# A decode step with two branches on one core: another cut of w_out, another way of turning the attention's output, another store

## The chip, the cores and the metric

The kernel runs on one core of a Trainium2 chip. The metric is the device time of one execution in microseconds (us); the figure for a kernel is the median of its runs. One further execution is recorded by the hardware profiler, and all durations below come from that one.

## The reference

One token (x, 1 x 576) goes through a layer norm and then through two branches in parallel; their results are added to x.

```python
xn = layernorm(x)
# branch A: cached attention, 32 query heads, 16 key/value heads of 128, the last W = 4096 positions
q = xn @ wq                                   # 576 x 4096
p = softmax(q k^T * 128**-0.5); o = p v       # two query heads share one k and v
A = o.reshape(4096) @ wo                      # 4096 x 576
# branch B: gated MLP
z = gelu(xn @ w_in)                           # 576 x 4608
g = w_sp * layernorm(z[2304:]) + b_sp         # one token: w_sp and b_sp are one number each
B = (z[:2304] * g) @ w_out                    # 2304 x 576
out = x + A + B
```

All inputs and the output are bfloat16. Some 51 MB are read from memory, most of it k and v.

## The kernel before, in words

Everything is loaded once, by SP, in the order of the list `order` (L105): w_q, the k and v of pairs of heads ("k0" to "k7", "v0" to "v7", 2 MB each), w_in in three pieces, and between and behind them w_o in four pieces ("wo0" to "wo3") and w_out. Eight buffers (`units`) are shared by all these loads, so a load waits for the release of an old buffer, and the issue lies well ahead of the landing. The schedule is written by hand: each engine runs its instructions in the order of the program text.

The list ends with "v6", "v7", "wout1", "wo3", "wout2". `wout_parts` (L104) cuts w_out, whose 2304 rows are held as 18 rows per partition: "wout1" is rows 0 to 7, "wout2" three pieces with rows 8 to 13, 14 to 16 and 17.

Heads are worked on in four groups (j = 0 to 3) of two pairs. `T` transposes k on PE (TensorE), `S` forms scores, `sm_max`, `sm_tr`, `sm_exp` and `sm_rec` the softmax, `PV` the products with v into `o_ps` (128 x 512, four blocks of 128 columns; a row has its own values in one of the four blocks). The loop over j and t (L468) puts the steps of three groups into each other, then `parts` places `turn`, `O_perm` and `WO` of earlier groups between the steps of the softmax.

`turn(j)` (L305) brings `o_ps` into the layout in which heads are columns: DVE copies it to `ov`, four fp32 products with columns of the 0/1 matrix `grp` pick the right rows of each block and add them up in `ot`, and DVE multiplies by the softmax's reciprocal sums into `oTn`. `O_perm(j)` (L316) spreads this over the partitions as w_o's rows lie (eight products, a masked product and a reduction on DVE), giving `oP`. `WO(j)` (L332) multiplies by one piece of w_o: 24 products with one column each, through `out_mm` (L327). `out_mm` adds into `out_ps`, whose three rows, on partitions 0, 32 and 64, hold 192 of the 576 outputs each.

`z_all`, `gelu`, `z_gate` and `z_rows` compute branch B up to `hv`, the vector that w_out multiplies; `hv` is there long before the end.

The end of the program (L509 to L523): the last eight steps of `PV`, rows 0 to 3 of w_out, `turn(3)`, rows 4 to 7, `O_perm(3)`, `WO(3)`, rows 8 to 17; then DVE copies the 65 partitions 0 to 64 of `out_ps` to `res`, and SP stores partitions 0, 32 and 64 of it, 384 bytes each.

Of the kernel before, what the change touches and what calls it, by code (L numbers as in the profile page):

```python
# [8 lines left out]
FP32 = mybir.dt.float32  # L9
BF16 = mybir.dt.bfloat16  # L10
ALU = mybir.AluOpType
# [3 lines left out]
P = 128  # L15
D = 576
HQ = 32
HKV = 16
DH = 128
# [10 lines left out]
NCG = 3  # L30
OW = D // NCG
PW = 28
NWO = 4
FR = FH // P
# [6 lines left out]
def kernel(  # L41
# [14 lines left out]
    nc = tc.nc  # L56
    ctx.enter_context(tc.manual_schedule())

    const = ctx.enter_context(tc.tile_pool(name="const", bufs=1))
    work = ctx.enter_context(tc.tile_pool(name="work", bufs=2))  # L60
# [14 lines left out]
    kn, vn, wq_t, win_t, wo_t, wout_t = {}, {}, {}, {}, {}, {}  # L75
# [25 lines left out]
        wo_t[j] = t  # L101

    win_parts = {1: (0, 3), 2: (3, 6), 3: (6, 9)}
    wout_parts = {1: (0, 8), 2: (8, 14, 17, 18)}  # L104
    order = ["wq1", "k0", "k1", "wq2", "k2", "k3", "v0", "v1", "win1", "win2", "win3", "k4", "k5", "v2", "v3", "wo0",  # L105
             "k6", "k7", "v4", "v5", "wo1", "wo2", "v6", "v7", "wout1", "wo3", "wout2"]
    for what in order:
        name, n = what.rstrip("0123456789"), what[-1]
# [45 lines left out]
    out_ps = ps_c.tile([P, OW], FP32, name="out_ps")  # L154
# [8 lines left out]
    for j in range(NS):  # L163
# [11 lines left out]
                                   op0=ALU.mult, op1=ALU.add, accum_out=stat[:, 1:2])  # L175
# [49 lines left out]
    o_ps = ps_o.tile([P, 4 * DH], FP32, name="o_ps")  # L225
# [67 lines left out]
    def PV(m):  # L293
        b, k = divmod(m, NCH // 2)
        j, i = divmod(b, 2)
        for g in range(4):
            w = 8 * g + 4 * i + k
            t = 4 * (4 * k + g)
            nc.tensor.matmul(o_ps[32 * g:32 * g + 32, :], lhsT=pz[j % 2][:, w, 16 - 16 * i:48 - 16 * i],  # L299
                             rhs=vn[b][:, t:t + 4, :].rearrange("p t d -> p (t d)"), start=i == 0 and k == 0,  # L300
                             stop=i == 1 and k == 3, skip_group_check=True, tile_position=(0, 32 * g))
# [1 line left out]


    def turn(j):  # L305
        ov = work.tile([P, 4 * DH], FP32, name=f"ov{j}", tag="ov")
        nc.vector.tensor_copy(ov[:], o_ps[:])  # L307
        ot = ps_m.tile([P, 8], FP32, name=f"ot{j}", tag="m")
        for t in range(4):
            nc.tensor.matmul(ot[:].rearrange("p (i c) -> p i c", i=2), lhsT=ov[:, DH * t:DH * (t + 1)],  # L310
                             rhs=grp[:].rearrange("p (i t c) -> p t i c", i=2, t=4)[:, t], start=t == 0, stop=t == 3)
        with nc.allow_low_precision(reason="the attention's output is bfloat16 in the reference"):
            nc.vector.tensor_tensor(out=oTn[:, 8 * j:8 * j + 8], in0=ot[:], in1=sm[j]["rm"][:], op=ALU.mult)  # L313

    def O_perm(j, n=1):
        op = ps_m.tile([P, 8, 8 * n], FP32, name=f"op{j}", tag="m")  # L316
        for r in range(8):
            nc.tensor.matmul(op[:, r, :], lhsT=selr[:, r, :, :].rearrange("p n q -> p (n q)"),
                             rhs=oTn[:, 8 * j:8 * j + 8 * n], start=True, stop=True)
        for k in range(n):  # L320
            tmp = work.tile([P, 8, 8], FP32, name=f"om{j + k}", tag="om")
            nc.vector.tensor_tensor(out=tmp[:], in0=op[:, :, 8 * k:8 * k + 8], in1=hm[:].unsqueeze(1).to_broadcast([P, 8, 8]), op=ALU.mult)
            with nc.allow_low_precision(reason="one of the eight is not zero, and it is a bfloat16 value"):
                nc.vector.tensor_reduce(out=oP[:, j + k, :], in_=tmp[:], axis=AXX, op=ALU.add)  # L324

    def out_mm(lhsT, rhs, start=False, last=False):
        for g in range(NCG):  # L327
            nc.tensor.matmul(out_ps[32 * g:32 * g + 1, :], lhsT=lhsT, rhs=rhs[:, OW * g:OW * (g + 1)],  # L328
                             start=start, stop=last, tile_position=(0, 32 * g))

    def WO(j):
        for r in range(8):  # L332
            out_mm(oP[:, j, r:r + 1], wo_t[j][:, D * r:D * (r + 1)])


    hv = const.tile([P, FR], BF16, name="hv")
# [74 lines left out]
    for n in range(NCH):  # L411
# [4 lines left out]
    grp = const.tile([P, 32], FP32, name="grp")  # L416
    nc.vector.tensor_reduce(out=grp[:], in_=ident_f[:].rearrange("p (g x) -> p x g", g=4), axis=AXX, op=ALU.add)
    sel = const.tile([P, 8], FP32, name="sel")
    nc.vector.tensor_reduce(out=sel[:].rearrange("p (i c) -> p i c", i=2),
                            in_=grp[:].rearrange("p (i t c) -> p i c t", i=2, t=4), axis=AXX, op=ALU.add)  # L420
    sel_neg = const.tile([P, 8], FP32, name="sel_neg")
    nc.vector.tensor_scalar(out=sel_neg[:], in0=sel[:], scalar1=1.0, scalar2=-NEG, op0=ALU.subtract, op1=ALU.mult)
    sel_t = const.tile([8, P], FP32, name="sel_t")
# [29 lines left out]
    for g in range(NCG):  # L453
        nc.tensor.matmul(out_ps[32 * g:32 * g + 1, :], lhsT=one_bf[:, 0:1], rhs=x_row[:, OW * g:OW * (g + 1)],
                         start=True, stop=False, tile_position=(0, 32 * g))
# [12 lines left out]
    for j in range(1, NB // 2):  # L468
# [23 lines left out]
        for k, what in enumerate(parts[j - 1]):  # L492
            if what == "z":
                z_all()
            elif what == "perm0":
                O_perm(0, 2)
            elif what == "perm2":
                O_perm(2)
            elif what[:4] == "turn":
                turn(int(what[4]))  # L500
            else:
                WO(int(what[2]))
            if k == 0:
                sm_exp(j)
            elif k == 1:
                sm_rec(j)
            if what == "z":
                G, sz = gelu()
    for m in range(NCH * 3, NCH * 4):  # L509
        PV(m)  # L510
    for r in range(4):
        out_mm(hv[:, r:r + 1], wout_t[r])
    turn(3)
    for r in range(4, 8):
        out_mm(hv[:, r:r + 1], wout_t[r])
    O_perm(3)
    WO(3)
    for r in range(8, FR):
        out_mm(hv[:, r:r + 1], wout_t[r], last=r == FR - 1)

    res = const.tile([P, OW], BF16, name="res")
    nc.vector.tensor_copy(res[0:32 * NCG - 31, :], out_ps[0:32 * NCG - 31, :])
    nc.sync.dma_start(out.flatten_outer_dims().rearrange("o (g c) -> (o g) c", g=NCG), res[0:32 * NCG - 31:32, :])  # L523


# [28 lines left out]
```

## Time and profile before

| what | value |
|---|---|
| median of 3 runs | 129.73 us (129.59 to 129.79) |
| the profiled execution | 129.77 us, its span 128.02 us |
| busy: PE, PE's weight loads, DVE, ACT | 68%, 48%, 47%, 23% |
| loads | 51 MB, mean 399 GB/s over the span |
| mean granted clock of TensorE | 0.85 |
| store: issue to the end of the span | 125.14 to 128.02 us |

The span is the time from the first to the last instruction in the trace; the execution's own time is 1.75 us longer. PE is TensorE, DVE is VectorE, ACT is ScalarE, SP is the engine that issues the loads and the store. In a timeline line the columns are start, length, engine, line, operation, result and sources, count; the bracket gives the idle time of the engine before it and what ended it.

### The profile page before, as it was taken

What the parts mean: (1) busy time and instruction counts of PE and PEld (TensorE: products, weight loads), DVE (VectorE), ACT (ScalarE), POOL (GpSimd) and SP (SyncE); (2) the same over time, 40 slices, a digit from 0 to 9 for tenths busy, and PEclk for the clock granted to TensorE, in tenths of its full rate; (3) what the DMA queues carried; (4) which work ended last, traced back from release to release, by engine and by line L of the source; (5) the groups of instructions that cost most, each with busy time, mean ns of one, the idle gap of its engine ahead of it and who ended that gap; (6) DMA issues with size and microseconds to landing.
All of it is one profiled execution on the core that took longest, in us unless ns stands there. A gap on an engine that the chain in (4) does not pass through costs nothing.

```text
span 128.0 us, 2605 instructions
## 1 busy us (share of the span) xinstructions
PE 86.7 (68%) x1141; PEld 61.3 (48%) x1141; DVE 60.2 (47%) x157; ACT 29.7 (23%) x39; POOL 10.2 (8%) x12
## 2 busy tenths in 40 slices
PE   2110996678895973247519969965999994697870
PEld 2110596634773621112319947624795643652640
DVE  6867157853679651002363675553365543402100
ACT  4000057320553410001200373512055432000000
POOL 7994000000000000000000000000000000000000
PEclk9999999999999999655555699999599999757755
DMA  4999999999999999999999999999999999999930
GB/s 123 430 394 445 430 451 388 436 420 450 430 415 412 433 410 436 445 405 430 461 420 410 415 427 427 435 440 415 420 425 415 423 437 425 425 414 420 400 133 0
DMA packets 4486, 51.11 MB, mean 399 GB/s; under 512 B 507, under 2 KB 636, under 8 KB 1020
## 3 DMA queue, kind: packets, MB, share of 16 engines
q1 hardware_dynamic: 4470, 50.96, 94.6%
q8 instruction: 9, 0.15, 0.5%
q10 hardware_dynamic: 6, 0.00, 0.0%
q14 instruction: 1, 0.01, 0.0%
HBM read 50.96 MB, written 0.00 MB: 398 GB/s over the span
## 4 chain that ended last, share of the span: by engine, by line
DMA 40%; PE 34%; DVE 15%; ACT 6%; issue 2%; POOL 0%; POOLq 0%; SPq 0%
DMA win<-in_B_w_in_dram 22%; PE tp L233 16%; DMA wout<-in_B_w_out_dram 15%; ACT kT L235 4%; DMA ws<-in_B_w_sp_dram 4%; PE s L250 3%; PE out_ps L328 3%; PE ot L310 2%; PE o_ps L299 2%; DVE ident_f L132 2%; DVE kT L237 2%; PE q_ps L343 1%; DVE twice L159 1%; PE za L343 1%; ACT p L275 1%
## 5 line engine op out<-in xcount | busy, mean ns | idle before, releaser
L233 PE MATMUL tp<-ident,k 128*128 128x128 bf16 x512 | 36.8, 233 | 3.6 <-ACT kT L235 1.9
L233 PEld LDWEIGHTS <-k 128*128 128x128 bf16 x512 | 33.0, 105 | 9.7 <-issue 9.6
L237 DVE COPY kT<-tp 128x1024 bf16<-128x1024 bf16 x40 | 27.0, 688 | 18.0 <-PE tp L233 17.7
L235 ACT COPY kT<-tp 128x1024 bf16<-128x1024 bf16 x24 | 23.9, 1012 | 41.3 <-PE tp L233 41.3
L299 PE MATMUL o_ps<-v,pz 128*32 128x512 bf16 x128 | 13.0, 442 | 1.4 <-DMA v<-in_A_v_cache_dram 1.4
L250 PE MATMUL s<-kT,qz 128*32 128x512 bf16 x128 | 11.4, 384 | 0.0
L310 PE MATMUL ot<-grp,ov 128*128 128x8 f32 x32 | 5.1, 286 | 7.1 <-DVE ov L307 7.1
L343 PEld LDWEIGHTS <-xe 128*2 128x2 bf16 x81 | 2.7, 94 | 14.6 <-issue 8.3
L343 PE MATMUL za<-win,xe 128*2 128x512 bf16 x36 | 4.8, 537 | 6.8 <-DMA win<-in_B_w_in_dram 6.8
L310 PEld LDWEIGHTS ot<-grp,ov 128*128 128x128 f32 x32 | 4.7, 227 | 7.6 <-issue 4.5
L299 PEld LDWEIGHTS <-pz 128*32 128x32 bf16 x128 | 4.2, 106 | 4.6 <-issue 3.2
L328 PE MATMUL out_ps<-wo,oP 128*1 128x192 bf16 x96 | 5.2, 331 | 1.3 <-DVE oP L324 0.7
L353 DVE COPY zr<-za 128x512 f32<-128x512 f32 x1 | 0.7, 691 | 11.0 <-PE za L343 11.0
L343 PE MATMUL q_ps<-wq,xe 128*2 128x512 bf16 x36 | 3.1, 486 | 3.9 <-DVE q_ps L408 3.9
L275 ACT ACTIVATE p<-s,nb 128x512 bf16<-128x512 f32 x4 | 2.8, 688 | 12.0 <-DVE nb L272 12.0
L307 DVE COPY ov<-o_ps 128x512 f32<-128x512 f32 x4 | 2.7, 682 | 5.0 <-PE o_ps L299 5.0
L250 PEld LDWEIGHTS <-qz 128*32 128x32 bf16 x128 | 3.3, 95 | 3.8 <-issue 0.7
L256 DVE TENSOR_REDUCE mx<-s 128x1 f32<-128x512 f32 x4 | 2.8, 692 | 4.9 <-PE s L250 4.9
L328 PEld LDWEIGHTS <-oP 128*1 128x1 bf16 x96 | 3.3, 107 | 2.2 <-DVE oP L324 1.4
L328 PE MATMUL out_ps<-wout,hv 128*1 128x192 bf16 x54 | 2.8, 306 | 1.6 <-DMA wout<-in_B_w_out_dram 1.6
L354 ACT COPY zr<-zb 2x256 f32<-2x256 f32 x1 | 0.4, 362 | 14.4 <-PE zb L343 14.4
L313 DVE TENSOR_TENSOR oTn<-ot,rm 128x8 bf16<-128x8 f32 x4 | 0.7, 167 | 6.1 <-PE ot L310 6.1
(117 smaller groups left out, 73.6 us busy)
## 6 DMA issues: line engine op xcount, KB each, us to landing
v<-in_A_v_cache_dram SPq DMA_DIRECT2D x8, 2048.0 KB, 27.0
k<-in_A_k_cache_dram SPq DMA_DIRECT2D x7, 2048.0 KB, 30.5
win<-in_B_w_in_dram SPq DMA_DIRECT2D x3, 1728.0 KB, 26.9
wo<-in_A_wo_dram SPq DMA_DIRECT2D x4, 1152.0 KB, 19.4
wq<-in_A_wq_dram SPq DMA_DIRECT2D x2, 2048.0 KB, 13.6
k<-in_A_k_cache_dram SPq DMA_DIRECT2D x2, 1024.0 KB, 11.3
wout<-in_B_w_out_dram SPq DMA_DIRECT2D x1, 1152.0 KB, 20.8
wout<-in_B_w_out_dram SPq DMA_DIRECT2D x1, 864.0 KB
```

The costliest lines, as they stand in the source:

```text
L132: nc.vector.tensor_copy(ident_f[:], ident[:])
L233: nc.tensor.transpose(tp[:, i, :], kn[b][:, 8 * c + i, :], ident[:])
L235: nc.scalar.copy(kT[n][:], tp[:])
L237: nc.vector.tensor_copy(kT[n][:], tp[:])
L250: nc.tensor.matmul(s_ps[j][32 * g:32 * g + 32, :], lhsT=qz[:, b, PW - 4 * v:PW - 4 * v + 32], rhs=kT[NCH * b + w // 2][:, 4 * (w % 2):4 * ...
L256: nc.vector.tensor_reduce(out=mx[:], in_=s_ps[j][:], axis=AXX, op=ALU.max)
L275: nc.scalar.activation(p[:], s_ps[j][:], ACT.Exp, bias=nb[:, 0:1], scale=SCALE, accum_out=ss[:])
L299: nc.tensor.matmul(o_ps[32 * g:32 * g + 32, :], lhsT=pz[j % 2][:, w, 16 - 16 * i:48 - 16 * i], rhs=vn[b][:, t:t + 4, :].rearrange("p t d - ...
L307: nc.vector.tensor_copy(ov[:], o_ps[:])
L310: nc.tensor.matmul(ot[:].rearrange("p (i c) -> p i c", i=2), lhsT=ov[:, DH * t:DH * (t + 1)], rhs=grp[:].rearrange("p (i t c) -> p t i c", ...
L328: nc.tensor.matmul(out_ps[32 * g:32 * g + 1, :], lhsT=lhsT, rhs=rhs[:, OW * g:OW * (g + 1)], start=start, stop=last, tile_position=(0, 32 ...
L343: nc.tensor.matmul(to[g // 4][32 * (g % 4):32 * (g % 4) + 2, 0:n], lhsT=xe_of(r), rhs=w[:, 512 * g:512 * g + n], start=first, stop=last, s ...
```

## The change

w_out is cut at rows 10, 15 and 17 instead of 8, 14 and 17. `turn` no longer copies `o_ps`: DVE multiplies each of the four blocks with a per-partition 0/1 mask (`own_t`, a new constant made from `grp`) and adds them up, and one fp32 product with `sel` replaces the four. At the end, `turn(3)` and `O_perm(3)` come directly behind `PV`, then rows 0 to 9 of w_out, `WO(3)`, and rows 10 to 17. The three rows of `out_ps` are copied one by one into one partition, the first and the third by ACT and the second by DVE, and SP stores one row of 1152 bytes.

```diff
-    wout_parts = {1: (0, 8), 2: (8, 14, 17, 18)}
+    wout_parts = {1: (0, 10), 2: (10, 15, 17, 18)}
...
     def turn(j):
-        ov = work.tile([P, 4 * DH], FP32, name=f"ov{j}", tag="ov")
-        nc.vector.tensor_copy(ov[:], o_ps[:])
+        ov = work.tile([P, DH], FP32, name=f"ov{j}", tag="ov")
+        nc.vector.tensor_scalar_mul(ov[:], o_ps[:, 0:DH], own_t[:, 0:1])
+        for t in range(1, 4):
+            nc.vector.scalar_tensor_tensor(out=ov[:], in0=o_ps[:, DH * t:DH * (t + 1)], scalar=own_t[:, t:t + 1],
+                                           in1=ov[:], op0=ALU.mult, op1=ALU.add)
         ot = ps_m.tile([P, 8], FP32, name=f"ot{j}", tag="m")
-        for t in range(4):
-            nc.tensor.matmul(ot[:].rearrange("p (i c) -> p i c", i=2), lhsT=ov[:, DH * t:DH * (t + 1)],
-                             rhs=grp[:].rearrange("p (i t c) -> p t i c", i=2, t=4)[:, t], start=t == 0, stop=t == 3)
+        nc.tensor.matmul(ot[:], lhsT=ov[:], rhs=sel[:], start=True, stop=True)
...
+    own_t = const.tile([P, 4], FP32, name="own_t")
+    nc.vector.tensor_reduce(out=own_t[:], in_=grp[:].rearrange("p (i t c) -> p t i c", i=2, t=4),
+                            axis=mybir.AxisListType.XY, op=ALU.add)
...
     for m in range(NCH * 3, NCH * 4):
         PV(m)
-    for r in range(4):
+    turn(3)
+    O_perm(3)
+    for r in range(10):
         out_mm(hv[:, r:r + 1], wout_t[r])
-    turn(3)
-    for r in range(4, 8):
-        out_mm(hv[:, r:r + 1], wout_t[r])
-    O_perm(3)
     WO(3)
-    for r in range(8, FR):
+    for r in range(10, FR):
         out_mm(hv[:, r:r + 1], wout_t[r], last=r == FR - 1)
 
-    res = const.tile([P, OW], BF16, name="res")
-    nc.vector.tensor_copy(res[0:32 * NCG - 31, :], out_ps[0:32 * NCG - 31, :])
-    nc.sync.dma_start(out.flatten_outer_dims().rearrange("o (g c) -> (o g) c", g=NCG), res[0:32 * NCG - 31:32, :])
+    res = const.tile([1, D], BF16, name="res")
+    for g in range(NCG):
+        copy = nc.vector.tensor_copy if g == 1 else nc.scalar.copy
+        copy(res[:, OW * g:OW * (g + 1)], out_ps[32 * g:32 * g + 1, :])
+    nc.sync.dma_start(out.flatten_outer_dims(), res[:])
```

## The prediction

> **What bounds the kernel now.** I read the page first: the DMA line of the 40 slices is at 9 from slice 2 to slice 38, so the load stream sets the pace, and only the tail behind it can shorten the time. The chain of waits, read next, ends so:
>
> ```profile
> 103.89 18.92 DMA wout<-in_B_w_out_dram
> 122.81 0.04 issue
> 122.85 1.88 PE out_ps L328 x26
> 124.73 0.02 issue
> 124.75 0.35 DVE res L522
> ```
>
> Columns: start, length, what. A piece of w_out, queued since 103.89, lands at 122.81. PE then works through 30 products, DVE copies the sum, and SP stores it. The timeline of the tail shows the clock and the order:
>
> ```profile
> 117.08 0.69 DVE L307 COPY ov<-o_ps 128x512 f32<-128x512 f32 x1 [4.99 <-PE o_ps L299]
> 117.91 0.50 PE L328 MATMUL out_ps<-wout,hv 128*1 128x192 bf16 x12 [0.88 <-DMA wout<-in_B_w_out_dram]
> ...
> 118.34 1.06 PE L310 MATMUL ot<-grp,ov 128*128 128x8 f32 x8
> ...
> 120.70 1.45 PE L328 MATMUL out_ps<-wo,oP 128*1 128x192 bf16 x24 [0.59 <-DMA wo<-in_A_wo_dram]
> ...
> 122.85 1.85 PE L328 MATMUL out_ps<-wout,hv 128*1 128x192 bf16 x30 [0.70 <-DMA wout<-in_B_w_out_dram]
> ...
> 124.75 0.35 DVE L522 CAST res<-out_ps 65x192 bf16<-65x192 f32 x1 [4.13 <-PE out_ps L328]
> 125.14 0.84 SPq L523 DMA_DIRECT2D out_dram<-res  x1
> ```
>
> The reader should see that PE waits three times for loads (brackets), and that the final 30 products need 0.053 us each (12 needed 0.035 at 117.91). The granted clock is 1.00 from 116.93 to 120.34 and 0.50 from there on. Landings, from the issue times and the times to landing of the DMA view: w_out's rows 0 to 7 at 117.87, wo3 at 120.66, rows 8 to 13 at 122.81, 14 to 16 at 123.86, row 17 at 124.25. So PE, ending at 124.70, is 0.45 behind the last load.
>
> After that the store: issue from 125.14 to 125.98; its three 384-byte packets run at 126.58 to 126.62; the last completion mark comes at 126.95; the closing barrier ends at 128.02. The store's 1.82 us from issue to completion is all on the path. The only one-partition transfers in the trace are loads, issued by ACT:
>
> ```profile
> 0.80 0.49 ACTq L72 DMA_DIRECT2D x_row<-in_A_x_dram  x1
> ```
> ```profile
> 25.31 0.21 ACTq L451 DMA_DIRECT2D ws<-in_B_w_sp_dram  x1
> ```
>
> Second column: the issue's length. x_row is one row of 1152 bytes, exactly the new store's shape; ws is 2 bytes.
>
> **The pieces.** The bytes are the same, so the last landing stays. The slowest DMA engine moves 8 of a piece's 128 packets, and a packet takes 51 ns for 1152 bytes, 139 for 3456, 264 for 6912, 349 for 9216: about 37 ns per 1000 bytes. The new packets (11520, 5760, 2304, 1152 bytes) are then 434, 221, 94 and 51 ns. Counting from v7's landing at 115.09: rows 0 to 9 at 118.56, wo3 at 121.36 (0.70 later), rows 10 to 14 at 123.13, 15 and 16 at 123.88, row 17 at 124.27. SP's queue keeps its order, and w_out's and wo3's issues lie 17 us or more ahead of their landings, so no issue becomes late.
>
> **turn(3).** Removed: one copy of 0.69 on DVE and eight product passes (four fp32 products) of 1.06. Added: four DVE passes of 128x128, each waiting for the one before. The nearest rows: a 128x512 copy at 0.684 and a 128x2 copy at 0.153 give 1.04 ns per element; a scalar read per partition adds 0.06 (L278 with one, 0.230, against L422 with none, 0.171). The first pass is 0.153 + 0.131 + 0.06 = 0.34. A scalar_tensor_tensor of 128x8 (L258) is 0.227, with 120 more elements 0.35. Sum: 0.34 + 3 x 0.35 + 3 x 0.03 between them = 1.5 us. Bounds: 1.15 (four bare copies) to 1.9 (half rate on the two-source passes, an estimate). From 117.08 the sums end at 118.6. One fp32 product is two passes: 0.32 to 0.61 by L270 and L283; I take 0.5, so 119.1. Then oTn and O_perm's eight products, 0.6 by the rows of before: 119.7. PE queues behind that wait everything that is left: ten rows of w_out, WO(3), the last rows. They landed at 118.56, so they start at 119.7 and need 1.05 at the full clock, 1.6 at half: 121.3 at the latest. wo3 lands at 121.36, so nothing is lost yet. WO(3) takes 1.45 and ends at 122.8, before rows 10 to 14 land at 123.13. The cover is 0.3 us there. Because wout's first rows no longer run while DVE copies, PE idles 1.5 us after PV; this cover hides it. If the sums took over 2 us, the excess would go to the end in full.
>
> **The last rows.** 24 products in place of 30, from 123.17: the last starts at 123.17 + 23 x 0.053 = 124.40, and row 17's landing allows 124.27 + 0.04 + 0.11 = 124.42. Before, the thirtieth started at 122.85 + 29 x 0.053 = 124.40. PE ends 0.02 later: two fewer rows, but a later landing.
>
> **Turns 0 to 2 and own_t.** Each earlier turn puts some 0.8 us more on DVE and takes some 0.5 off PE; su, pt and pz of sm_rec queue behind it. The load stream hides this: PV(28) has to wait for v7 at 115.09, and PV of v6, 1.75 us from 112.91, leaves 0.4 free. own_t is one reduction (L419, smaller out, took 0.206) at about 13 us, where k's loads set the pace. I cost all of it at nothing; without that cover turn(2) would cost 0.1 to 0.3.
>
> **The copies.** DVE's one copy of 0.35 becomes two in a row on ACT, with one on DVE beside them; SP waits for both engines. ACT's nearest is its 2x256 copy out of PSUM, 0.362; at 0.84 ns per element (1012 ns for 1024) 192 elements are 0.31. Two ACT instructions in a row overlap by 0.10 (p at 88.53 for 0.69, its accumulator read already at 89.11), so 0.52: +0.17. The upper bound is two of 0.362 without overlap: +0.37. The Trainium skill, ScalarE: Activation LUTs, What ACT_TABLE_LOAD costs, gives 186 ns + 0.833 ns per element and 93 ns of overlap, which would make it 0.60 and +0.25. The row here, 0.362 for 256, is below its 0.40; by that rule the forecast would be 129.48.
>
> **The store.** One row instead of three. By x_row: issue 0.49 instead of 0.84 (-0.35); from the issue's end to the first packet 0.39 instead of 0.60 (-0.20); one packet of 1152 bytes, +0.03; completion 0.29 to 0.31 behind the data in both. Sum -0.52. Bounds: by ws the issue is 0.21, -0.27 more; above, no gain at all, because the trace has no other store and 0.84 may belong to a store rather than to its three rows. I take x_row, the row of the same shape.
>
> **Sum.** 129.77 (the profiled execution; its span is 128.02, and 1.75 lies around it) + 0.02 + 0.17 - 0.52 = 129.44. The median of the three runs, 129.73, lies 0.04 below that execution, so 129.40 for a median.
>
> **Rivals.** (1) The store costs the same whatever its shape, and the copies are paid: 129.73 + 0.02 + 0.17 to 0.37 = 129.92 to 130.12, slower. It decides where the store gains less than the copies cost, 0.17. For it: SP issues 128-row loads in 0.33 us, so rows alone do not make 0.84. Against: two one-row issues are at 0.21 and 0.49, and no load anywhere has three rows. The Trainium skill speaks for this rival: DMA: Bandwidth & Descriptors, Anatomy of one DMA, says that the fixed cost is mostly waiting for the write's receipt, not setup. Here the trace disagrees: 0.84 of 1.82 us is the issue, and 0.31 the wait behind the data. 0.25.
>
> (2) The store gains only part, about as much as the copies cost: 129.7. An x_row issued by ACT at the start may not price SP at the end. 0.12.
>
> (3) The masked sums take over 2 us: WO(3) starts late, the last rows with it, 129.9 to 130.3. For: four dependent passes, PSUM read each time. Against: it needs 0.5 more than the rows give. 0.06.
>
> (4) PE's clock is full at the end: the last rows end right behind the landing, at 124.5, and the time is 129.2. The clock returned to 1.00 only behind windows full of wide products (113.5 to 116.9); one-column products did not bring it. 0.05.
>
> The likeliest case has 0.52, its own range 129.1 to 129.6.
>
> **How the numbers follow.** A measurement of this kernel can tell about 0.2%, 0.26 us. Faster than 129.47: all of (4) and most of the likeliest, 0.55. Slower than 129.99: two thirds of (1), and (3), 0.23. Between: 0.22. The range goes from the likeliest with ws's issue, 129.1, to (1)'s upper end, 130.1.
>
> **What would show it.** Right: SP's store of L528 at some 0.5 us or less; two ACT copies of L527 at 0.3 that together span 0.5; PE's last product at 124.7 by that profile's span; four DVE passes of about 0.35 behind PV; WO(3) waiting for wo3, and the last 24 products waiting for w_out. Wrong: a store issue still at 0.8; ACT copies of 0.36 or more one behind the other; WO(3) or the last rows waiting for DVE's oP instead of a load; a different clock from 120 on.

## The result, and the profile after

The changed kernel takes 129.25 us (median of 8 runs, 129.18 to 129.46), the kernel before on the same chip 129.69 (8 runs, 129.59 to 129.87). The ratio is 0.9967, interval 0.9957 to 0.9978: 0.44 us faster, where 0.33 was forecast, and inside the range.

The profiled execution took 129.26 us with a span of 127.43, before 129.77 and 128.02. The timeline of its tail (start, length, engine, line, operation, count; in brackets the idle time before and what ended it):

```profile
117.26 0.35 DVE L307 TENSOR_SCALAR ov<-o_ps,own_t 128x128 f32<-128x128 f32 x1 [4.17 <-PE o_ps L299]
117.65 1.12 DVE L309 SCALAR_TENSOR_TENSOR ov<-o_ps,own_t,ov 128x128 f32<-128x128 f32 x3
...
118.92 0.36 PE L312 MATMUL ot<-sel,ov 128*128 128x8 f32 x2 [1.71 <-DVE ov L309]
...
119.81 1.76 PE L329 MATMUL out_ps<-wout,hv 128*1 128x192 bf16 x30
...
121.37 1.49 PE L329 MATMUL out_ps<-wo,oP 128*1 128x192 bf16 x24
...
123.09 1.35 PE L329 MATMUL out_ps<-wout,hv 128*1 128x192 bf16 x24 [0.24 <-DMA wout<-in_B_w_out_dram]
...
124.49 0.35 DVE L527 CAST res<-out_ps 1x192 bf16<-1x192 f32 x1 [4.08 <-PE out_ps L329]
124.52 0.63 ACT L527 CAST res<-out_ps 1x192 bf16<-1x192 f32 x2 [15.47 <-PE out_ps L329]
125.18 0.32 SPq L528 DMA_DIRECT2D out_dram<-res  x1
```

The reader should see three things. PE idles 1.71 us behind PV, waiting for the masked sums, and the last 24 products still wait for a load, not for DVE: the cover held. `WO(3)`, at 121.37, has no bracket: it follows rows 0 to 9 directly and doesn't wait for wo3. The two ACT copies fill 0.63 us, nearly twice DVE's old copy of 0.35. The store's issue is 0.32 instead of 0.84.

The end of the chain of waits (start, length, what) shows the last piece of w_out, not DVE, as what PE followed:

```profile
106.11 17.67 DMA wout<-in_B_w_out_dram
123.78 0.04 issue
123.82 0.33 PE out_ps L329 x6
124.16 0.04 issue
124.20 0.30 PE out_ps L329 x3
124.52 0.31 ACT res L527
```

Rows 15 and 16 start at 123.82, with the landing of their piece at 123.78; row 17 starts at 124.20, with its landing at 124.16.

### The profile page after: what moved, and what is told of

The parts are those of the page before. It is cut to its first block, busy times and chain, and to the rows that moved or that the text cites. A ratio compares the mean times of both kernels' runs of the same rounds, so it can differ in the third digit from the quotient of the medians.

```text
span 127.4 us, 2574 instructions
## 1 busy us (share of the span) xinstructions
PE 83.7 (66%) x1117; PEld 59.4 (47%) x1117; DVE 63.0 (49%) x170; ACT 30.4 (24%) x41; POOL 10.2 (8%) x12
## 4 chain that ended last, share of the span: by engine, by line
DMA 39%; PE 33%; DVE 17%; ACT 6%; issue 2%; POOL 0%; ACTq 0%; POOLq 0%; SPq 0%
DMA win<-in_B_w_in_dram 22%; PE tp L233 17%; DMA wout<-in_B_w_out_dram 14%; DMA ws<-in_B_w_sp_dram 4%; PE s L250 4%; ACT kT L235 3%; PE o_ps L299 2%; DVE kT L237 2%; DVE ov L309 2%; DVE ident_f L132 2%; PE out_ps L329 2%; PE q_ps L344 1%; DVE twice L159 1%; PE za L344 1%; ACT p L275 1%
## 5 line engine op out<-in xcount | busy, mean ns | idle before, releaser
L233 PE MATMUL tp<-ident,k 128*128 128x128 bf16 x512 | 37.7, 237 | 3.3 <-DVE kT L237 1.7
L233 PEld LDWEIGHTS <-k 128*128 128x128 bf16 x512 | 34.0, 108 | 9.4 <-issue 9.2
L299 PE MATMUL o_ps<-v,pz 128*32 128x512 bf16 x128 | 12.1, 416 | 1.4 <-DVE rem L213 1.4
L312 PE MATMUL ot<-sel,ov 128*128 128x8 f32 x8 | 1.9, 312 | 11.3 <-DVE ov L309 11.3
L312 PEld LDWEIGHTS ot<-sel,ov 128*128 128x128 f32 x8 | 1.6, 249 | 12.1 <-issue 7.3
L309 DVE SCALAR_TENSOR_TENSOR ov<-o_ps,own_t,ov 128x128 f32<-128x128 f32 x12 | 4.2, 351 | 0.4
L527 ACT CAST res<-out_ps 1x192 bf16<-1x192 f32 x2 | 0.6, 310 | 15.5 <-PE out_ps L329 15.5
L307 DVE TENSOR_SCALAR ov<-o_ps,own_t 128x128 f32<-128x128 f32 x4 | 1.4, 342 | 4.2 <-PE o_ps L299 4.2
```

The lines of the kernel that those rows point to most:

```text
L233: nc.tensor.transpose(tp[:, i, :], kn[b][:, 8 * c + i, :], ident[:])
L309: nc.vector.scalar_tensor_tensor(out=ov[:], in0=o_ps[:, DH * t:DH * (t + 1)], scalar=own_t[:, t:t + 1], in1=ov[:], op0=ALU.mult, op1=ALU.add)
L312: nc.tensor.matmul(ot[:], lhsT=ov[:], rhs=sel[:], start=True, stop=True)
```

## The experiments

Ratios are against the kernel before on the same chip, with their 95% interval.

**The new end alone** (the kernel before, with the last lines of the change):

```diff
-    res = const.tile([P, OW], BF16, name="res")
...
+    res = const.tile([1, D], BF16, name="res")
+    for g in range(NCG):
+        copy = nc.vector.tensor_copy if g == 1 else nc.scalar.copy
+        copy(res[:, OW * g:OW * (g + 1)], out_ps[32 * g:32 * g + 1, :])
+    nc.sync.dma_start(out.flatten_outer_dims(), res[:])
```

> The kernel before with the new end alone: three copies of one row each (two on ACT, one on DVE) and a store of one row; turn, pieces and order as before. Theory A (the store's shape makes the gain): the store's issue falls from 0.84 to about 0.32 us and the copies grow from 0.35 to about 0.63, PE's last product stays at about 0.45 us behind the last landing; 0.4 us faster than before, about 129.3. Rival B (the gain comes from the new order at the end, which brings PE's full clock back): no more than 0.2 us faster, 129.5 to 129.7.

129.42 us, 0.9975 (0.9965 to 0.9986). In the profile PE's last product ends 0.41 behind the last landing (124.01), before 0.45, at a clock of 0.50 in both; the copies take 0.63, and the issue 0.32:

```profile
124.49 0.63 ACT L524 CAST res<-out_ps 1x192 bf16<-1x192 f32 x2 [15.66 <-PE out_ps L328]
125.14 0.32 SPq L525 DMA_DIRECT2D out_dram<-res  x1
```

Three quarters of the gain are there, without the new order. With the next run, which has the order and not the end, rival B is out.

**All but the new end** (the changed kernel with the old copy and store):

```diff
-    res = const.tile([1, D], BF16, name="res")
...
+    res = const.tile([P, OW], BF16, name="res")
+    nc.vector.tensor_copy(res[0:32 * NCG - 31, :], out_ps[0:32 * NCG - 31, :])
+    nc.sync.dma_start(out.flatten_outer_dims().rearrange("o (g c) -> (o g) c", g=NCG), res[0:32 * NCG - 31:32, :])
```

> The changed kernel with the old end: one copy of 65 partitions on DVE and a store of three rows. Theory A: store's issue at 0.84 again, 129.6 to 129.75, within 0.1 of the kernel before. Rival B: PE's clock at 1.00 behind the last landing, 129.3 to 129.5.

129.63 us, 0.9993 (0.9978 to 1.0007): no difference that can be told. The store's issue is at 0.84 again:

```profile
124.90 0.84 SPq L526 DMA_DIRECT2D out_dram<-res  x1
```

The two ratios multiply to 0.9968, the whole change's 0.9967: the parts add up, as far as the intervals can tell.

**Four rows.** Why are three rows dear? The same end as in the last kernel, with four rows of 144:

```diff
-NCG = 3
+NCG = 4
```

> The changed kernel with out_ps in four rows of 144 instead of three of 192, one DVE copy of 97 partitions and a store of four rows of 288 bytes. If three rows are dear because of the number three, four rows are issued in about 0.33 us, the copy takes 0.30 in place of 0.63, and the time is about 128.95. If any store of several rows is dear, its issue is 0.8 or more and the time 129.4 or above. If short rows are dear for the memory, the mark of completion comes later than 0.3 us behind the packets.

129.43 us, 0.9973 (0.9962 to 0.9983). The issue is 0.65, between the two readings, and the copy 0.31:

```profile
124.89 0.31 DVE L525 CAST res<-out_ps 97x144 bf16<-97x144 f32 x1 [4.22 <-PE out_ps L329]
125.23 0.65 SPq L526 DMA_DIRECT2D out_dram<-res  x1
```

Four rows cost less than three, so the price doesn't grow with the rows, but they aren't cheap either. The packets, of 288 bytes, run at 126.48 to 126.55, 0.60 behind the issue's end, as with 384 bytes; no wait for short rows is seen.

**Shapes of small transfers.** The changed kernel with nine more transfers behind the copies:

```diff
+    nc.scalar.dma_start(ov_[:, 0:24], pst[0:1, 0:24])
+    nc.scalar.dma_start(ov_[:, 24:72].rearrange("o (g c) -> (o g) c", g=2), pst[0:2, 0:24])
+    nc.scalar.dma_start(ov_[:, 72:144].rearrange("o (g c) -> (o g) c", g=3), pst[0:3, 0:24])
...
+    nc.scalar.dma_start(pld[0:16, 108:144], xv[:, 0:576].rearrange("o (g c) -> (o g) c", g=16))
```

> The changed kernel with nine more small transfers, issued by ACT behind its two copies and ahead of SP's store, which waits for them: stores of 1, 2, 3, 4 and 8 rows of 48 bytes, then loads of 1, 3, 4 and 16 rows of 72 bytes. Its time is not compared; the issue of each shape is. If the price lies in the number of rows not being a power of two, 3 rows take about 0.8 us and 2, 4, 8 and 16 about 0.3 to 0.65 and 1 row 0.2 to 0.3, in stores and loads alike. If it lies in storing, the loads are at 0.2 to 0.35 whatever their rows. If it grows with the rows, 8 and 16 are dearest.

In the timeline L533 to L537 are stores of 1, 2, 3, 4 and 8 rows:

```profile
124.94 0.24 ACTq L533 DMA_DIRECT2D out_dram<-pst  x1
...
125.52 0.27 ACTq L535 DMA_DIRECT2D out_dram<-pst  x1
125.82 0.28 ACTq L536 DMA_DIRECT2D out_dram<-pst  x1
126.14 0.31 ACTq L537 DMA_DIRECT2D out_dram<-pst  x1
```

The loads take 0.26 to 0.32. All three readings that were written down fell: neither the number three, nor storing, nor many rows is dear where the rows lie side by side, as here. What is left of the old store's shape is that its rows lay on partitions 0, 32 and 64.

**The step between partitions.** The same with eight other transfers:

```diff
+    nc.scalar.dma_start(ov_[:, 0:72].rearrange("o (g c) -> (o g) c", g=3), pst[0:3, :])
+    nc.scalar.dma_start(ov_[:, 72:144].rearrange("o (g c) -> (o g) c", g=3), pst[0:65:32, :])
+    nc.scalar.dma_start(ov_[:, 144:240].rearrange("o (g c) -> (o g) c", g=4), pst[0:97:32, :])
...
+    nc.sync.dma_start(pld[0:65:32, 192:384], xv.rearrange("o (g c) -> (o g) c", g=3))
```

> The changed kernel with eight more small transfers ahead of its store: from ACT, stores of 3 rows on neighbouring partitions, then of 3, 4 and 2 rows that lie 32 partitions apart; from SP, stores of 3 rows side by side and 32 apart, then loads of 3 rows of 384 bytes side by side and 32 apart. Its time is not compared. If the step of 32 partitions is what made three rows 0.84 and four 0.65, the issues with the step take that and those without it 0.27, on both engines. If it is SP, all of SP's are at 0.6 to 0.85 and all of ACT's at 0.27. If it is the place at the end behind a long wait, none is.

ACT's three rows side by side (L533), then three, four and two with the step of 32:

```profile
123.81 0.28 ACTq L533 DMA_DIRECT2D out_dram<-pst  x1
...
124.13 0.81 ACTq L534 DMA_DIRECT2D out_dram<-pst  x1
124.98 0.56 ACTq L535 DMA_DIRECT2D out_dram<-pst  x1
125.58 0.53 ACTq L536 DMA_DIRECT2D out_dram<-pst  x1
```

SP, which doesn't wait for ACT's copies and so issued its four earlier: stores of three rows side by side and 32 apart, then loads of the same two kinds:

```profile
108.06 0.34 SPq L537 DMA_DIRECT2D out_dram<-pst  x1
109.51 0.83 SPq L538 DMA_DIRECT2D out_dram<-pst  x1
114.38 0.26 SPq L539 DMA_DIRECT2D pld<-in_A_x_dram  x1
117.86 0.72 SPq L540 DMA_DIRECT2D pld<-in_A_x_dram  x1
```

The step is the price: 0.27 to 0.53 us more at issue, on both engines, in stores and in loads, at the end and in the middle. SP's four alternate, so it isn't the place in the sequence either. It also shows behind the issue: from the end of ACT's issue to the first packet it is 0.64 with the step and 0.48 without (0.48 to 0.49 for one to eight rows in the experiment before). With the step, three rows cost more than two or four (0.81 against 0.53 and 0.56); why is open. No other step than 32 was run.

**PE kept busy.** In the profile of the changed kernel the clock was 1.00 behind the last landing, in that of all but the new end 0.50, with the same order of products. Nine more products fill PE's wait for the sums; their result isn't used:

```diff
+        if j == 3:
+            fill = ps_t.tile([P, 512], FP32, name="fill", tag="tp")
+            for k in range(9):
+                nc.tensor.matmul(fill[:], lhsT=ident[:], rhs=wo_t[2][:, 0:512], start=True, stop=True)
```

> The changed kernel with nine more products of 128x512 in PE's idle time between PV and turn(3)'s product; their result is not used. Theory A (PE's clock at the end depends on how full the window before it is): PE is busy from 117 to 122.8, the clock is 1.00 behind the last landing whatever the phase of the clock's windows, PE ends within 0.35 us of the last landing, and the time is that of the changed kernel or up to 0.1 less, about 129.2. Rival (one-column products never keep the clock up): the clock at the end is 0.50 in some runs as before, the time the same, 129.25 to 129.35. If the added products delay turn(3), the time grows by their excess.

129.19 us, 0.9959 (0.9947 to 0.9971). The clock is at 1.00 from 117.99 to 124.81, and the copies start 0.33 behind the last landing. Against the changed kernel's 0.9967 that is no difference which can be told. The clock at the end is worth some 0.1 us: the copies start 0.33 behind the landing here and in the changed kernel, 0.43 and 0.45 behind it in all but the new end and in the changed kernel with the old turn, which have the same order of products and a clock of 0.50. The profile agrees with theory A, but it is one execution, and a full window alone isn't enough (see the windows below).

**The changed kernel with the old turn:**

```diff
-        nc.tensor.matmul(ot[:], lhsT=ov[:], rhs=sel[:], start=True, stop=True)
+        for t in range(4):
+            nc.tensor.matmul(ot[:].rearrange("p (i c) -> p i c", i=2), lhsT=ov[:, DH * t:DH * (t + 1)],
+                             rhs=grp[:].rearrange("p (i t c) -> p t i c", i=2, t=4)[:, t], start=t == 0, stop=t == 3)
```

> The changed kernel with the old turn (one copy, four fp32 products); pieces, order and store as changed. Theory A: turn(3) ends some 0.4 us earlier or at the same time, w_out's rows and WO(3) still wait for their loads; 129.25 to 129.35, the same as the changed kernel. Rival (the masked sums are what slowed the kernel with the new turn alone by 0.4%, and the change carries that loss too): faster than the changed kernel by 0.3 us or more, below 129.0.

129.26 us, 0.9963 (0.9950 to 0.9975): the changed kernel's time. In the changed kernel the masked sums neither gain nor lose anything that can be told.

**The new turn alone, twice** (the kernel before with the new `turn` and `own_t`; the same kernel in both):

```diff
+        for t in range(1, 4):
+            nc.vector.scalar_tensor_tensor(out=ov[:], in0=o_ps[:, DH * t:DH * (t + 1)], scalar=own_t[:, t:t + 1],
+                                           in1=ov[:], op0=ALU.mult, op1=ALU.add)
...
+        nc.tensor.matmul(ot[:], lhsT=ov[:], rhs=sel[:], start=True, stop=True)
```

> The kernel before with the new turn alone (masked sums, one product), the order of products, the pieces and the store as before. Theory A: the sums are 0.8 us longer than the copy, PE's products 0.7 shorter, w_out's rows run beside; oP is there before wo3 lands; 129.6 to 129.8, no difference that can be measured. Rival: the sums delay WO(3) and the last rows, 129.8 to 130.0.

> The kernel before with the new turn alone, a second time. In the first, median 130.20 with a range of 129.67 to 130.98, the profiled execution had a load stream 0.35 us late and 2.2 us outside the span in place of 1.75, and one block of instructions was fetched at 130.0, behind the end. If the loss comes from where the instructions lie, the profile again shows that fetch behind the end, some 2.2 us outside the span, and a median of 130.0 or more. If it was chance, the median is 129.7 to 129.85 and the time outside the span 1.75. If the sums themselves cost time, the span is longer and DVE or PE's wait for DVE stands in the chain at the end.

First 130.20 us, 1.0038 (1.0015 to 1.0061), then 129.83, 1.0016 (1.0001 to 1.0031): a miss of theory A. The second median lies in the range written down for chance, while the late fetch in its profile is what was written down for the place of the instructions, so the second set doesn't decide between the two. But the spans don't tell of a loss. They are 127.8 to 128.5 in the first set, with a median of 128.05, and before's on the same chip are mostly 127.8 to 128.2; what grows is the time outside the span. It is 1.7 to 1.9 us in every run of the other kernels that are compared by ratios here, and 1.7 to 3.1 in this one (130.93 us with a span of 127.8). Within the span its DMA view counts eight blocks of instructions, and the ninth is fetched at 130.0 and 129.0, behind the program's last instruction; in the kernel before it lies at 123.6.

```profile
q8 instruction: 8, 0.13, 0.4%
```

Before, the line is `q8 instruction: 9, 0.15, 0.5%`.

**The new turn alone, padded** with three more fp32 products per turn, which the real one overwrites:

```diff
+        for k in range(3):
+            nc.tensor.matmul(ot[:], lhsT=ident_f[:], rhs=sel[:], start=True, stop=True)
         nc.tensor.matmul(ot[:], lhsT=ov[:], rhs=sel[:], start=True, stop=True)
```

> The kernel before with the new turn alone, and in each turn three more fp32 products of the same form ahead of the real one, which overwrites them: PE's number of instructions is that of the kernel before again, the masked sums stay. If the loss of the new turn alone comes from where PE's instructions lie (a block fetched behind the program's end), the time outside the span is 1.7 to 1.9 us in every run, the last fetch lies at about 124, and the median is 129.65 to 129.8. If it comes from the sums or from DVE's instructions, the time outside the span again reaches 2 to 3 us in some runs and the median is 129.8 to 130.2.

129.78 us, 0.9999 (0.9987 to 1.0011); outside the span 1.7 to 1.9 us in all 11 runs, and the ninth block at 123.4:

```profile
q8 instruction: 9, 0.15, 0.5%
```

So the larger loss, of the first set, isn't the sums', which are all still there. The loss goes with the late block of instructions, in the three profiles of these two kernels; that the late fetch causes it isn't shown. In the second set's profile the fetch came at 129.0, and that execution had only 1.9 us outside its span; of the 24 runs of the new turn alone 15 have 1.7 to 1.9 us outside. What moves the block is open too: all but the new end has as many instructions on every engine as the new turn alone, and fetches it in time (124.3).

**Two stores**, the version that the runs pointed to: the fill, and ACT stores its second piece itself:

```diff
+    res2 = const.tile([1, OW], BF16, name="res2")
+    nc.scalar.copy(res2[:], out_ps[64:65, :])
...
+    nc.sync.dma_start(ov_[:, 0:2 * OW], res[:, 0:2 * OW])
+    nc.scalar.dma_start(ov_[:, 2 * OW:D], res2[:])
```

> The changed kernel with the nine products that fill PE's idle time (as in the fill experiment), and the store cut in two: SP stores the first two thirds as soon as ACT's first copy and DVE's copy are done, ACT itself stores the last third behind its second copy. SP's issue of 0.32 then lies beside ACT's second copy, and ACT's issue costs 0.24 and no signal to SP: 0.1 us less than the fill experiment, about 129.1. If the second store's completion comes later on ACT's queue than on SP's, or PE's and ACT's bookkeeping at the end grows, no gain: 129.2 to 129.3.

129.22 us, 0.9946 (0.9933 to 0.9960), the lowest ratio of all; the interval overlaps the changed kernel's and the fill's, so that it beats either isn't shown. In its profile SP's issue lies beside ACT's second copy, and ACT's, 0.23, ends at 125.56, 0.93 behind the start of the first copy, where the changed kernel's one issue ends 1.01 behind:

```profile
124.99 0.31 ACT L532 CAST res<-out_ps 1x192 bf16<-1x192 f32 x1
125.04 0.32 SPq L534 DMA_DIRECT2D out_dram<-res  x1
125.33 0.23 ACTq L535 DMA_DIRECT2D out_dram<-res  x1
```

Half of these 0.08 is lost again behind the issue: the last completion mark comes 1.77 behind the first copy's start, against 1.81. ACT's packet starts 0.49 behind the end of its issue, SP's 0.42 to 0.43.

## Why the prediction was right

What bounds the end, the cover for the sums and the signs of the terms for the copies and the store were forecast as they came. That the sum came so close is in part luck: the copies cost more, the store saved more and for another reason, and in the profiled execution PE had another clock than forecast.

**The pieces and the landings.** Forecast 118.56, 121.36, 123.13, 123.88 and 124.27; measured 118.47, 121.26, 123.05, 123.78 and 124.16. v7, from which they were counted, was itself 0.08 earlier, so the packet arithmetic holds to 0.03.

**turn(3).** The sums: 1.5 forecast, 117.26 to 118.77 measured; single passes 0.342 and 0.351 against 0.34 and 0.35. The product 0.36, within the bounds and below the 0.5 taken. The first rows start at 119.81 (119.7 forecast), WO(3) ends at 122.86 (122.8), before rows 10 to 14 land. The cover of 0.3 was 0.2 in that execution. One sign did not come: WO(3) didn't wait for wo3. Rows 0 to 9 took 1.76 at a clock of 0.50, where 1.6 was reckoned, so WO(3) started at 121.37, 0.11 behind wo3's landing; in all but the new end, where these rows ran at 1.00 in 1.04, it did wait, 0.64. Rival (3) didn't occur, and the old turn in the changed kernel gives the same time.

**The last rows: the wrong reason about the clock.** Forecast +0.02; the first copy started 0.27 earlier (124.49 instead of 124.75). Of this 0.09 is the earlier landing, some 0.1 the clock, 1.00 from 123.08 on (by the profiles of the same order at 0.50, above), and the rest, less than 0.1, probably the two fewer rows, which no run had alone. Rival (4)'s effect, a different clock from 120 on, which the prediction names among the signs of its being wrong, was there in that execution. The chance of that rival, 0.05, rested on the reading that only windows full of wide products had brought the clock back. That was wrong. The windows of the clock in the changed kernel (columns: window, length, busy time and count of PE, of its weight loads, of DVE, ACT and POOL, then granted clock, DMA share and GB/s):

```profile
116.25:119.66 3.41, 1.44 (x26) 0.68 (x16) 1.57 (x5) 0.00 (x0) 0.00 (x0) 1.00 1.00 412
119.66:123.08 3.42, 3.20 (x62) 2.50 (x60) 0.45 (x2) 0.00 (x0) 0.00 (x0) 0.50 0.82 325
123.08:124.60 1.52, 1.16 (x24) 0.66 (x23) 0.11 (x1) 0.08 (x1) 0.00 (x0) 1.00 0.17 58
```

A window filled to 0.94, nearly all of it with one-column products, was followed by 1.00. The kernel before had shown it already: its window from 89.62 to 93.03 is full, with 24 one-column products (`WO`) among 39, and 1.00 follows:

```profile
89.62:93.03 3.41, 3.40 (x39) 2.66 (x40) 1.25 (x6) 0.00 (x0) 0.00 (x0) 0.50 1.02 432
93.03:96.44 3.41, 3.04 (x51) 2.79 (x49) 2.63 (x4) 2.11 (x3) 0.00 (x0) 1.00 0.96 404
```

In all but the new end the window was filled to 0.71, and the clock stayed at 0.50:

```profile
120.37:123.78 3.41, 2.43 (x48) 1.68 (x42) 0.00 (x0) 0.00 (x0) 0.00 (x0) 0.50 0.70 269
```

Same products, another place of the windows. How full a window is by the profile doesn't decide alone: in the new end alone the window from 67.05 is full, and the clock stayed at 0.50:

```profile
67.05:70.46 3.41, 3.41 (x27) 3.41 (x28) 1.29 (x4) 0.00 (x0) 0.00 (x0) 0.50 1.00 423
70.46:73.88 3.42, 3.42 (x34) 3.42 (x32) 2.02 (x6) 1.13 (x2) 0.00 (x0) 0.50 1.01 426
```

What decides is open. The Trainium skill, TensorE: Matmul & The Clock Gate, Part 1, says that windows of 3413 ns run freely and don't begin with the kernel; the traces agree, with windows of 3.41 us that begin at 119.66 here and 120.37 there. No gain of the new order is seen over many runs: all but the new end is at 0.9993. How often the clock is full at the end, the profiles, one of each kernel, don't tell.

**The copies: too small.** Forecast +0.17; measured +0.31 (from the first copy's start to the store's issue 0.69 instead of 0.38). A copy is 0.31 as reckoned. The step that failed is the overlap of 0.10, taken from an exponential and the reading of its sum; the two copies start at 124.52 and 124.84 and don't overlap at all. In the kernel before, copies on ACT overlap by 0.10 too, two of 1.01 in 1.91:

```profile
74.41 1.91 ACT L235 COPY kT<-tp 128x1024 bf16<-128x1024 bf16 x2
```

So the rows allowed the overlap, and why these two copies have none is open; in the experiment with two stores, where they write two tiles, they have none either (124.66 and 124.99). The Trainium skill's figures (ScalarE: Activation LUTs, What ACT_TABLE_LOAD costs) gave 0.60 for the pair; the pair took 0.63, but by a shorter copy (0.31 against the 0.35 that its rule gives for 192 elements) and no overlap, where it has 93 ns.

**The store: the right row, the wrong cause, and too small.** Forecast -0.52. From the issue's start to the last completion mark it is 125.18 to 126.30, 1.12 us instead of 1.82: -0.70. The issue fell by 0.52 (0.35 forecast: x_row's 0.49 is that of a load, issued by ACT at the program's start; SP's store is at 0.32, and which of these differences makes the rest was not run), and the time from the issue's end to the first packet from 0.60 to 0.42 (0.39 forecast). What the prediction put down to "one row instead of three" is the step of 32 partitions: three rows side by side are issued in 0.28 by ACT and 0.34 by SP. The time to the first packet goes with the step as well: 0.64 against 0.48 on ACT, and on SP at the end 0.60 with the step, for three rows and for four, against 0.42 for one row. A store of one row has no step, so the forecast came out on the right side by luck. Rival (1), a store that costs the same whatever its shape, is refuted by the issue, 0.32 instead of 0.84; the new end alone gains 0.25%, so rival (2), a store that gains no more than the copies cost, is out too. The passage of the Trainium skill that the prediction cites for rival (1) (DMA: Bandwidth & Descriptors, Anatomy of one DMA) is on the gpsimd path; this store is issued by SP, so the passage didn't speak for that rival here.

**The sum.** The start of the first copy -0.27, the copies +0.31, the store -0.70, and from the last completion mark to the end of the span +0.06 (1.13 instead of 1.07): together -0.60, and the span fell by 0.59. The execution's own time fell by 0.51, as 1.83 instead of 1.75 us lay outside, and the medians by 0.44. The new end alone is worth 129.78 - 129.42 = 0.36 by the medians; copies, store and closing make 0.33 by one profile.

## What to carry to other kernels

Where a store closes the kernel, its whole time from issue to completion is on the path, and here a store whose rows lay 32 partitions apart took 1.82 us, one without such a step 1.12. Bring the rows together before storing them, and count the copies that this costs (0.31 here). One partition was tried for the whole store; neighbouring partitions only for small transfers, by their issue. Price an operation that the trace doesn't show by a row of the same shape, but write down every way in which the two differ; here rows, step and engine had changed together, and the wrong one was named. When a part of a change seems to cost time, compare the spans with the times before looking for the cause in the program. And when a rule on the clock is read off a trace, look at every change of the clock in it: the kernel before had the exception to the one used here.

## What the runs showed of the hardware that was not expected

A transfer whose rows lie 32 partitions apart takes 0.53 (two rows), 0.81 (three) and 0.56 us (four) to issue from ACT, against 0.24 to 0.31 for one to eight rows side by side; a load of three rows from SP 0.72 against 0.26. The first packet follows the end of ACT's issue by 0.64 instead of 0.48 us.

Two runs of the same kernel with the same span can differ by over a microsecond outside it (129.68 us with 127.8, 130.93 with 127.8), in the new turn alone, the one kernel compared here whose profiles show the last block of instructions fetched behind its end. That the one causes the other isn't shown.

Two one-row ACT copies out of PSUM, one behind the other and into different columns, ran at 0.31 us each with 0.01 between them, where pairs of 128x1024 copies overlap by 0.10.
